# One-core attention with two feed-forward layers: value matmuls a step later, evacuations by kind, another order of the first two head pairs

## The chip, the cores and the metric

The kernel runs on one core of one Trainium2 chip. The metric is the device time of one execution in microseconds (us); for the kernel before it is the median of three runs. Engine names: TensorE (PE, its weight loads PEld), VectorE (DVE), ScalarE (ACT), GpSimd (POOL) and SyncE (SP), which here issues all DMA transfers from one queue (SPq).

## The reference

Four batches of eight heads are given, 576 positions, 64 channels a head, all float32. Queries and keys are rotated by position, attention is computed, and its output (2304 tokens by 512 channels) passes through two feed-forward layers of width 2048.

```python
def rotate(x):
    x1, x2 = (x[..., :half], x[..., half:])
    return np.concatenate([x1 * cos - x2 * sin, x1 * sin + x2 * cos], axis=-1)
...
scores = scale * np.matmul(rotate(q), rotate(k).transpose(0, 1, 3, 2))
scores = scores - np.max(scores, axis=-1, keepdims=True)
attn = np.exp(scores)
attn = attn / (np.sum(attn, axis=-1, keepdims=True) + 1e-09)
x = np.matmul(attn, v)             # then laid out as 2304 x 512
h = x @ w_in;  x = np.where(h > 0, h, np.exp(np.minimum(h, 0)) - 1) @ w_out
h = x @ w_in2; x = (h - np.tanh(h)) @ w_out2
```

## The kernel before, in words

**Two stages.** The attention stage handles 16 pairs of heads. The feed-forward stage (from L428) works through two layers in 192 steps. Both are written as loops whose program order is kept on each engine. The change lies in the attention stage, but for one constant (`NCV`) that both stages use.

**Items and steps.** A pair has nine items: eight score tiles of 128 queries by 576 keys (four tiles of each head), and a ninth that holds the last 64 queries of both heads. The main loop (L378) makes step i out of parts of different items. In its order, step i issues: the loads scheduled for i; `emit_max(i)`, the row maximum of score tile i (VectorE); `emit_s(i+1)`, the matmuls of the next score tile; `emit_exp(i)`, the exponential with its row sum (ScalarE); `flush()`, which copies to SBUF what the step before left in PSUM; `emit_norm(i-1)`, after every second item the reciprocals (VectorE) and the scaling of two tiles (GpSimd, L251); the `prep` parts scheduled for i; at some steps a part of a weight conversion (`conv_w`); `emit_t(i-4)`, four TensorE transposes, with one more for the remaining 64 columns (`pr`); and the value matmuls (`emit_pv`) that fall due, as `PV_AT` says, one, two or three steps after their last transposes. In this text "step r of a pair" counts i modulo nine.

**Buffers that tie steps together.** Score tiles have two PSUM buffers, so `emit_s(i+1)` waits for the exponential of item i-1. Transposes have three PSUM buffers and the value result has one. Normalised tiles have three SBUF buffers; rotated inputs `t`, keys `k` and values have two.

**Preparing a pair.** `load_qk(p, x)` loads queries (x=0) or keys (x=1) with their swapped halves into `t` (576 KB in one transfer). `prep(p, x, i)` then has five parts: i=0 and 1 multiply the two halves by the tables (GpSimd; for pair 0 and half of pair 1 VectorE); 2 adds them (VectorE, L148); 3 makes the rounded high part (ScalarE, L151); 4 makes the low part (VectorE, L156) and issues the copies that `place` makes of both parts: four of 288 KB for keys (`k<-hl`), four of 144 KB for queries (`qa<-hl`, `qb<-hl`). The score matmuls of a pair read these copies. Only the first `NDIRECT` score tiles read the rotated float32 tiles directly (L193). `when` and `early` say in which step each load and part is issued. Rotated tiles have two buffers each, so the tiles of pair 2 take the place of those of pair 0.

**Weights.** `load_w` loads a 512 KB block of raw 8-byte weights, `conv_w` turns it into two float32 parts: ScalarE takes an absolute value, VectorE makes four instructions, ScalarE and GpSimd split the result. One block is converted in every two pairs.

**Evacuations.** `evac` notes copies of transposes to SBUF (nine of 512 columns and five of 128 or 64 in each pair), and `flush` gives two of every five to VectorE and the others to ScalarE, by a running count, whatever their size.

Of the kernel before, what the change touches and what calls it, by code (L numbers as in the profile page):

```python
# [8 lines left out]
F32 = mybir.dt.float32  # L9
# [3 lines left out]
ALU = mybir.AluOpType  # L13
# [10 lines left out]
def attention_elu_tanhshrink(ctx: ExitStack, tc: tile.TileContext, qk, v, w1i, w1o, w2i, w2o, tab, out):  # L24
# [6 lines left out]
    nc = tc.nc  # L31
    NPAIR = qk.shape[0]
    NTOK, DM = out.shape
    S = 576
    NB = 384
    SCALE = 0.125
# [31 lines left out]
        raw_t[key] = t  # L68

    cv_t = {}  # L70
    NCV = 5

    def conv_w(key, slot, part):
        l, kind, c = key
        if part < 4:
            words = raw_t[key].bitcast(U32).rearrange("p (n t) -> p n t", t=2)
            lo_w, hi_w = words[:, :, 0], words[:, :, 1]
        if part == 0:
            cv_t[key] = cv_p.tile([128, 512], F32, tag="f", name="f")
        f = cv_t[key]  # L80
        fu = f.bitcast(U32)
        if part == 0:
            nc.scalar.activation(out=f, in_=hi_w.bitcast(F32), func=AF.Abs)
        elif part == 1:
            nc.vector.tensor_scalar(out=f, in0=f, scalar1=LO_CLAMP, scalar2=HI_CLAMP, op0=ALU.max, op1=ALU.min)
            nc.vector.tensor_scalar(
                out=fu, in0=fu, scalar1=3, scalar2=0x3FFFFFFF, op0=ALU.logical_shift_left, op1=ALU.bitwise_and
            )
        elif part == 2:
            nc.vector.scalar_tensor_tensor(  # L90
                out=fu, in0=hi_w, scalar=0xC0000000, in1=fu, op0=ALU.bitwise_and, op1=ALU.bitwise_or
            )
        elif part == 3:
            nc.vector.scalar_tensor_tensor(
                out=fu, in0=lo_w, scalar=29, in1=fu, op0=ALU.logical_shift_right, op1=ALU.bitwise_or
            )
            raw_t.pop(key)
        else:
            w = w_pools[slot // 4 if slot < 4 else -1].tile(
                [128, 2, 512], F32R, tag=f"w{kind}_{slot}", name=f"w{kind}_{slot}"  # L100
            )
            nc.scalar.copy(out=w[:, 0, :], in_=f)  # L102
            nc.gpsimd.tensor_tensor(out=w[:, 1, :], in0=f, in1=w[:, 0, :].bitcast(F32), op=ALU.subtract)  # L103
            w_t[key] = w
            cv_t.pop(key)


    with ExitStack() as actx:
# [27 lines left out]
        def prep(p, x, i):  # L136
            t = t_t[p, x]
            mul = SCALE if p > 0 and x == 0 else 1.0
            if i < 2:
                if p == 0 and x == 0:  # L140
                    nc.vector.scalar_tensor_tensor(
                        out=t[:, i, :], in0=t[:, i, :], scalar=SCALE, in1=tabs[:, i, :], op0=ALU.mult, op1=ALU.mult
                    )
                else:
                    eng = nc.vector if p < 2 and i == 1 else nc.gpsimd
                    eng.tensor_tensor(out=t[:, i, :], in0=t[:, i, :], in1=tabs[:, i, :], op=ALU.mult)  # L146
            elif i == 2:
                nc.vector.tensor_tensor(out=t[:, 0, :], in0=t[:, 0, :], in1=t[:, 1, :], op=ALU.add)  # L148
            elif i == 3:
                hl_t[p, x] = p1.tile([128, 2, S], F32R, tag=f"hl{x}", name=f"hl{x}")  # L150
                nc.scalar.mul(hl_t[p, x][:, 0, :], t[:, 0, :], mul)  # L151
            else:
                hl = hl_t.pop((p, x))
                if p > 0:
                    t_t.pop((p, x))
                nc.vector.scalar_tensor_tensor(  # L156
                    out=hl[:, 1, :], in0=t[:, 0, :], scalar=mul, in1=hl[:, 0, :].bitcast(F32),
                    op0=ALU.mult, op1=ALU.subtract,
                )
                if p == 0 and x == 0:  # L160
                    first_hl.append(hl)
                for h in range(2):
                    if p > 0:
                        place(p, x, h, hl)
                    elif x == 1:
                        place(p, 0, h, first_hl[0])
                        place(p, 1, h, hl)

        first_hl = []

        def place(p, x, h, hl):
            src = hl[64 * h:64 * h + 64].bitcast(F32)
# [79 lines left out]
                    out=a, in0=a, scalar1=r[:, x:x + 1], scalar2=1.0, op0=ALU.mult, op1=ALU.mult  # L252
                )

        ev = [0]
        late, late_x = [], []

        def evac(out_, in_):
# [1 line left out]

        def flush():
            for out_, in_ in late:
                ev[0] += 1
                if ev[0] % 5 in (1, 3):
                    nc.vector.tensor_copy(out_, in_)  # L265
                else:
                    nc.scalar.copy(out_, in_)  # L267
            late.clear()
            for p, grp, o, n in late_x:
                b, hp = divmod(p, 4)  # L270
                x0 = NTOK * hp + b * S + 256 * grp
                nc.scalar.copy(out=xa[:, x0:x0 + n], in_=o[:, 0:n])
            late_x.clear()
# [58 lines left out]
                late_x.append((p, min(grp, 1), o_t.pop((p, min(grp, 1))), 256 if grp == 0 else 320))  # L332

        D = 4
        NDIRECT = 2
        NI = 9
        first_w = [(0, kind, c) for c in range(NJ) for kind in range(2)]
        sched = {}
        early = {1: ((None, 0, 0, 1, 2, 3), (None, 0, 0, 0, 1, 2)), 2: ((0, 4, 5, 7, 7, 8), (4, 7, 9, 11, 12, 13))}
        for p in range(1, NPAIR):  # L340
            i0 = NI * (p - 1)
            for x in range(2):
# [3 lines left out]
                if when[0] is not None:  # L346
                    sched.setdefault(when[0], []).append((load_qk, p, x))
                for k in range(5):
                    sched.setdefault(when[k + 1], []).append((prep, p, x, k))
            sched.setdefault(i0 + 7, []).append((load_v, p))  # L350
        with tc.manual_schedule():
            for x in range(2):
                t = t_t[0, x] = p2.tile([128, 2, S], F32, tag=f"t{x}", name=f"t{x}")
                for i in range(2):
                    nc.sync.dma_start(out=t[:, i, :], in_=qk[0, :, 2 * x + i, :])
                    if x == 0:
                        nc.sync.dma_start(out=tabs[:, i, :], in_=tab[:, i, :])
            load_qk(1, 0)
            load_qk(1, 1)
            load_v(0)  # L360
            make_identity(nc, ident)
            nc.vector.memset(zero, 0.0)
            for i in range(2):
                nc.scalar.copy(out=qa_t[i][:, S:640], in_=zero)
                nc.scalar.copy(out=qb_t[i][:, 0:64], in_=zero)
            for i in range(3):
                prep(0, 0, i)
            for i in range(3):
                prep(0, 1, i)
            n = len(items)  # L370
            pend = []
            nw = list(range(len(first_w)))[::-1]
            emit_s(0)
            PV_AT = ((1, 1, 1, 3, 3), (1, 1, 1, 3, 3), (2, 2, 2, 2, 2))
            for i in range(3, 5):
                for x in range(2):
                    prep(0, x, i)
            for i in range(n + D + 1):  # L378
                p, r = divmod(i, NI)
                for f, *arg in sched.get(i, ()):  # L380
# [13 lines left out]
                if p < NPAIR:  # L394
                    for f, *arg in sched.get(i, ()):
                        if f is prep:
                            f(*arg)
                    c = NI * (p % 2) + r - 3
                    if c >= 0 and c % 2 == 0 and c // 2 < NCV and p // 2 < len(first_w):
                        key = first_w[p // 2]  # L400
                        conv_w(key, key[2], c // 2)
                if 0 <= i - D < n:
                    emit_t(i - D)
                    pp, uu, hh = items[i - D]
# [214 lines left out]
```

## Time and profile before

| what | us |
|---|---|
| median of three runs (1132.15 to 1132.97) | 1132.17 |
| profiled execution, its own time | 1132.65 |
| span of that execution in the trace | 1130.9 |
| PE busy in the span | 1097.3 |
| DVE busy | 765.6 |
| ACT busy | 688.6 |
| POOL busy | 671.3 |

The span runs from the first to the last instruction of the trace; the execution's own time has 1.75 us more around it. Busy times are sums over instructions. A busy PE is not PE at its peak, since the ends of pipelined matmuls are modelled. Times in the rows below count from the start of the span.

### The profile page before, as it was taken

Reading aid. Unit: us, or ns where it says so; the run is one execution under the profiler, and the core shown is the slowest. Engines: PE = TensorE matmul, PEld = TensorE weight load, DVE = VectorE, ACT = ScalarE, POOL = GpSimd, SP = SyncE. Lnnn points to the kernel's source line nnn. Section 1 sums busy time; section 2 is a strip of 40 time slices with the busy share of each in tenths; the row PEclk is TensorE's granted clock in tenths of the full one; section 3 lists DMA queues with packets and bytes.
Section 4 is the critical chain, followed back from the end, with each engine's and each line's share of the span. In section 5 each row is a group of like instructions: output and inputs, shape, how many; then the busy total and the mean of one; then the engine's idle time right before and its main releaser. Section 6 shows DMA issues by size and latency. Waiting matters only on the chain.

```text
span 1130.9 us, 18518 instructions
## 1 busy us (share of the span) xinstructions
PE 1097.3 (97%) x6656; PEld 987.2 (87%) x6656; DVE 765.6 (68%) x1393; ACT 688.6 (61%) x1477; POOL 671.3 (59%) x609
## 2 busy tenths in 40 slices
PE   2899999999999999999999999999999999999998
PEld 2777776777799999999999999998998899899987
DVE  6988888888645434555545556678768877877665
ACT  3676766676745533333333344688888788877774
POOL 2877887887556533333333466676666666666443
PEclk9999999999999999999999999999999999999999
DMA  7767676865211111112111121111111111110102
GB/s 232 217 193 200 181 215 169 222 172 164 72 39 38 40 55 38 38 38 55 40 38 38 38 57 38 39 38 38 57 38 38 38 56 38 38 39 1 57 35 78
DMA packets 29627, 91.96 MB, mean 81 GB/s; under 512 B 4192, under 2 KB 4192, under 8 KB 29536
## 3 DMA queue, kind: packets, MB, share of 16 engines
q1 hardware_dynamic: 29536, 90.78, 28.3%
q8 instruction: 53, 0.87, 0.3%
q14 instruction: 38, 0.31, 0.1%
HBM read 57.74 MB, written 4.72 MB: 55 GB/s over the span
## 4 chain that ended last, share of the span: by engine, by line
PE 90%; DVE 5%; DMA 2%; ACT 2%; SPq 1%; issue 1%; ACTq 0%; DVEq 0%
PE h L445 36%; PE y L503 18%; PE y L505 17%; PE o L325 8%; PE s L211 6%; PE pt L291 4%; DVE nm L220 2%; DMA k<-hl 1%; ACT a L234 1%; DVE t L148 1%; DVE aT L265 1%; ACT aT L267 1%; DVE hl L156 0%; DMA tabs<-in_tab 0%; PE pr L304 0%
## 5 line engine op out<-in xcount | busy, mean ns | idle before, releaser
L445 PE MATMUL h<-x,w 128*128 128x384 f32 x2304 | 434.0, 336 | 0.0
L445 PEld LDWEIGHTS h<-x,w 128*128 128x128 f32 x2304 | 407.1, 188 | 8.0 <-ACT a L234 0.4
L488 POOL TENSOR_TENSOR g<-f,g 128x384 fp32r<-128x384 f32 x192 | 213.6, 1113 | 187.8 <-ACT g L487 182.5
L503 PE MATMUL y<-g,w 128*128 128x384 f32 x1152 | 219.0, 339 | 0.0
L505 PE MATMUL y<-w,g 128*128 128x512 f32 x864 | 216.7, 395 | 0.2 <-ACT xa L520 0.2
L503 PEld LDWEIGHTS y<-g,w 128*128 128x128 f32 x1152 | 204.0, 188 | 0.0
L505 PEld LDWEIGHTS y<-w,g 128*128 128x128 f32 x864 | 161.5, 188 | 31.9 <-ACT xa L520 0.6
L251 POOL TENSOR_SCALAR a<-a,r 128x576 f32<-128x576 f32 x144 | 135.2, 951 | 63.7 <-DVE r L248 43.6
L464 POOL TENSOR_TENSOR w<-w,u 128x384 f32<-128x384 f32 x96 | 105.4, 1098 | 99.7 <-ACT w L463 99.7
L234 ACT ACTIVATE a<-s,nm 128x576 f32<-128x576 f32 x144 | 107.1, 743 | 89.6 <-DVE nm L220 75.1
L487 ACT CAST g<-f 128x384 fp32r<-128x384 f32 x192 | 98.0, 510 | 94.1 <-PE y L503 92.4
L475 DVE TENSOR_SCALAR f<-f 128x384 f32<-128x384 f32 x96 | 40.0, 416 | 145.4 <-ACT f L456 145.4
L456 ACT ACTIVATE f<-h 128x384 f32<-128x384 f32 x96 | 47.2, 492 | 146.7 <-PE h L445 143.8
L220 DVE TENSOR_REDUCE nm<-s 128x1 f32<-128x576 f32 x144 | 108.2, 753 | 38.1 <-PE s L211 36.5
L103 POOL TENSOR_TENSOR w<-f,w 128x512 fp32r<-128x512 f32 x64 | 82.6, 1291 | 54.4 <-ACT w L102 54.3
L522 DVE TENSOR_TENSOR xa<-y,xa 128x384 f32<-128x384 f32 (+1 forms) x126 | 74.0, 612 | 47.3 <-PE y L503 42.0
L479 DVE TENSOR_TENSOR f<-h,f 128x384 f32<-128x384 f32 x96 | 53.1, 553 | 68.3 <-ACT f L465 67.8
L481 DVE COPY_PREDICATED f<-mask,w 128x384 f32<-128x384 uint32 x96 | 92.2, 961 | 10.3 <-DVE w L480 0.5
L325 PE MATMUL o<-aT,v 128*64 128x256 f32 (+1 forms) x768 | 89.3, 339 | 2.6 <-ACT aT L267 2.4
L146 POOL TENSOR_TENSOR t<-t,tabs 128x576 f32<-128x576 f32 x59 | 86.3, 1463 | 8.2 <-DMA t<-in_qk 8.2
L291 PE MATMUL pt<-ident,a 128*128 128x128 f32 x576 | 88.3, 277 | 0.1
L461 ACT ACTIVATE u<-h 128x384 f32<-128x384 f32 x96 | 47.4, 494 | 66.4 <-PE h L445 52.1
(55 smaller groups left out, 1379.2 us busy)
## 6 DMA issues: line engine op xcount, KB each, us to landing
k<-hl SPq DMA_DIRECT2D x64, 288.0 KB, 4.2
t<-in_qk SPq DMA_DIRECT2D x30, 576.0 KB, 6.2
raw<-in_w1i SPq DMA_DIRECT2D x16, 512.0 KB, 3.7
raw<-in_w1o SPq DMA_DIRECT2D x16, 512.0 KB, 3.7
raw<-in_w2i SPq DMA_DIRECT2D x16, 512.0 KB, 3.6
raw<-in_w2o SPq DMA_DIRECT2D x16, 512.0 KB, 3.6
v<-in_v SPq DMA_DIRECT2D x16, 288.0 KB, 4.7
qa<-hl SPq DMA_DIRECT2D x32, 144.0 KB, 4.0
```

The costliest lines, as they stand in the source:

```text
L220: nc.vector.tensor_reduce(out=nm, in_=s_t[i][:, :, 0:288], axis=AX.XY, op=ALU.max, negate=True)
L234: nc.scalar.activation(out=a.rearrange("p (x c) -> p x c", x=2), in_=s[:, :, 0:288], func=AF.Exp, bias=nm_t.pop(i), scale=1.0, accum_out=den,)
L251: nc.gpsimd.tensor_scalar(out=a, in0=a, scalar1=r[:, x:x + 1], scalar2=1.0, op0=ALU.mult, op1=ALU.mult)
L291: nc.tensor.transpose(pt[:, c, :], a[:, h or 0, c0:c0 + 128], ident)
L325: nc.tensor.matmul(out=o[sl, 0:n], lhsT=w, rhs=m, start=(c == 0), stop=(c == 4))
L445: nc.tensor.matmul(out=hp, lhsT=w[:, wp, ws], rhs=x_t[t][:, xp, c, :], start=(m == 0), stop=(m == 3 * KC - 1))
L464: nc.gpsimd.tensor_tensor(out=w, in0=w, in1=u, op=ALU.mult)
L481: nc.vector.copy_predicated(f, mask.bitcast(U32), w)
L487: nc.scalar.copy(out=g[:, 0, :], in_=f)
L488: nc.gpsimd.tensor_tensor(out=g[:, 1, :], in0=f, in1=g[:, 0, :].bitcast(F32), op=ALU.subtract)
L503: nc.tensor.matmul(out=y_t[e][:, 0:NB], lhsT=w[:, wp, es], rhs=gt[:, gp, :], start=st, stop=sp)
L505: nc.tensor.matmul(out=y_t[e], lhsT=gt[:, gp, es], rhs=w[:, wp, :], start=st, stop=sp)
```

## The change

The value matmuls of each group are issued one step later (`PV_AT`), and the load of a pair's values three steps later. Evacuations of at most 128 columns go to VectorE, all larger ones to ScalarE. The part of `conv_w` that held two VectorE instructions is cut in two, and the parts get their own steps (`CV_AT`, counted in 18 steps, two pairs). In the first pair VectorE does all products and sums: keys first, then queries 0 to 319, and after the first score matmuls are issued the other 256 queries. Keys and the first 320 queries are loaded ahead of the rest. The first four score tiles instead of two read float32. All four products of pair 1 go to GpSimd ahead of the loop, and the loads of pair 2 move from steps 0 and 4 to steps 4 and 5, its query parts by a step or two.

```diff
-    NCV = 5
+    NCV = 6
...
             nc.vector.tensor_scalar(out=f, in0=f, scalar1=LO_CLAMP, scalar2=HI_CLAMP, op0=ALU.max, op1=ALU.min)
+        elif part == 2:
             nc.vector.tensor_scalar(
                 out=fu, in0=fu, scalar1=3, scalar2=0x3FFFFFFF, op0=ALU.logical_shift_left, op1=ALU.bitwise_and
             )
...
             if i < 2:
-                if p == 0 and x == 0:
-                    nc.vector.scalar_tensor_tensor(
-                        out=t[:, i, :], in0=t[:, i, :], scalar=SCALE, in1=tabs[:, i, :], op0=ALU.mult, op1=ALU.mult
-                    )
-                else:
-                    eng = nc.vector if p < 2 and i == 1 else nc.gpsimd
-                    eng.tensor_tensor(out=t[:, i, :], in0=t[:, i, :], in1=tabs[:, i, :], op=ALU.mult)
+                nc.gpsimd.tensor_tensor(out=t[:, i, :], in0=t[:, i, :], in1=tabs[:, i, :], op=ALU.mult)
...
-                if p == 0 and x == 0:
-                    first_hl.append(hl)
                 for h in range(2):
-                    if p > 0:
-                        place(p, x, h, hl)
-                    elif x == 1:
-                        place(p, 0, h, first_hl[0])
-                        place(p, 1, h, hl)
+                    place(p, x, h, hl)
+
+        def rotate_first(x, cols):
+
+            t = t_t[0, x][:, :, cols]
+            for i in range(2):
+                if x == 0:
+                    nc.vector.scalar_tensor_tensor(
+                        out=t[:, i, :], in0=t[:, i, :], scalar=SCALE, in1=tabs[:, i, cols], op0=ALU.mult, op1=ALU.mult
+                    )
+                else:
+                    nc.vector.tensor_tensor(out=t[:, i, :], in0=t[:, i, :], in1=tabs[:, i, cols], op=ALU.mult)
+            nc.vector.tensor_tensor(out=t[:, 0, :], in0=t[:, 0, :], in1=t[:, 1, :], op=ALU.add)
...
-                ev[0] += 1
-                if ev[0] % 5 in (1, 3):
+                if out_.free_size() <= 128:
                     nc.vector.tensor_copy(out_, in_)
                 else:
                     nc.scalar.copy(out_, in_)
...
-        NDIRECT = 2
+        NDIRECT = 4
+        Q0 = 320
+        CV_AT = (3, 5, 7, 9, 10, 13)
-        early = {1: ((None, 0, 0, 1, 2, 3), (None, 0, 0, 0, 1, 2)), 2: ((0, 4, 5, 7, 7, 8), (4, 7, 9, 11, 12, 13))}
+        early = {1: ((None, None, None, 3, 3, 4), (None, None, None, 1, 1, 2)), 2: ((4, 5, 6, 7, 8, 9), (5, 7, 9, 11, 12, 13))}
...
-            sched.setdefault(i0 + 7, []).append((load_v, p))
+            sched.setdefault(i0 + 10, []).append((load_v, p))
...
+            for i in range(2):
+                nc.sync.dma_start(out=t_t[0, 1][:, i, :], in_=qk[0, :, 2 + i, :])
+                nc.sync.dma_start(out=tabs[:, i, :], in_=tab[:, i, :])
+                nc.sync.dma_start(out=t_t[0, 0][:, i, 0:Q0], in_=qk[0, :, i, 0:Q0])
+            nc.sync.dma_start(out=t_t[0, 0][:, :, Q0:S], in_=qk[0, :, 0:2, Q0:S])
+            load_qk(1, 1)
             load_qk(1, 0)
-            load_qk(1, 1)
             load_v(0)
...
-            for i in range(3):
-                prep(0, 0, i)
-            for i in range(3):
-                prep(0, 1, i)
+            rotate_first(1, slice(0, S))
+            rotate_first(0, slice(0, Q0))
...
             emit_s(0)
-            PV_AT = ((1, 1, 1, 3, 3), (1, 1, 1, 3, 3), (2, 2, 2, 2, 2))
-            for i in range(3, 5):
-                for x in range(2):
-                    prep(0, x, i)
+            PV_AT = ((2, 2, 2, 4, 4), (2, 2, 2, 4, 4), (3, 3, 3, 3, 3))
+            rotate_first(0, slice(Q0, S))
+            for x in (1, 0):
+                for i in range(2):
+                    prep(1, x, i)
+            prep(0, 1, 3)
+            prep(0, 1, 4)
+            prep(0, 0, 3)
+            sched.setdefault(0, []).insert(0, (prep, 0, 0, 4))
...
-                    c = NI * (p % 2) + r - 3
-                    if c >= 0 and c % 2 == 0 and c // 2 < NCV and p // 2 < len(first_w):
-                        key = first_w[p // 2]
-                        conv_w(key, key[2], c // 2)
+                    key = first_w[p // 2]
+                    if i % (2 * NI) in CV_AT:
+                        conv_w(key, key[2], CV_AT.index(i % (2 * NI)))
```

## Rows read from the trace of the kernel before

**Rows 1.** Windows by stage: start:end, length, busy PE, PEld, DVE, ACT, POOL, clock, DMA

```profile
0.00:41.12 41.12, 17.57 (x89) 13.84 (x90) 28.36 (x48) 15.75 (x35) 17.95 (x21) 0.96 0.83 242
41.12:53.16 12.04, 12.04 (x109) 9.12 (x108) 11.15 (x23) 8.10 (x22) 11.77 (x12) 1.00 0.58 162
53.16:306.67 253.51, 247.53 (x2047) 187.75 (x2045) 211.64 (x481) 176.65 (x440) 200.97 (x186) 1.00 0.67 180
318.71:1130.90 812.19, 808.21 (x4317) 768.52 (x4317) 510.80 (x833) 482.96 (x967) 437.42 (x388) 1.00 0.14 42
```

**Rows 2.** Windows of three single pair periods, same columns

```profile
180.55:199.59 19.04, 17.62 (x148) 13.40 (x147) 16.52 (x36) 12.80 (x32) 16.30 (x16) 1.00 0.65 186
199.59:217.18 17.59, 17.59 (x148) 13.41 (x147) 14.58 (x36) 12.33 (x31) 13.09 (x12) 1.00 0.78 200
289.22:306.67 17.45, 17.45 (x149) 13.39 (x147) 11.94 (x32) 12.53 (x32) 11.12 (x13) 1.00 0.21 59
```

**Rows 3.** Timeline, PEld: ninth score tile of pairs 1 and 15 (16 such rows)

```profile
53.16 0.81 PEld L211 LDWEIGHTS s<-k,qb 128*128 128x128 f32 x6
...
306.67 0.81 PEld L211 LDWEIGHTS s<-k,qb 128*128 128x128 f32 x6
```

**Rows 4.** Chain of waits, 181 to 186 us: start, length, what

```profile
181.26 1.70 DVE f L90
...
182.96 0.68 DVE nm L220
...
183.67 0.83 ACT a L234 x2
...
184.50 0.48 ACT aT L267
...
185.03 1.51 PE o L325 x10
```

**Rows 5.** Waits of PEld, 40 to 308 us: total, times, longest

```profile
PEld o L325 <- ACT aT L267: 8.2, 14, 1.9
```

**Rows 6.** Timeline of the start: start, length, instruction (idle before, releaser)

```profile
7.73 1.99 DVE L148 TENSOR_TENSOR t<-t 128x576 f32<-128x576 f32 x1
...
9.77 3.75 POOL L146 TENSOR_TENSOR t<-t,tabs 128x576 f32<-128x576 f32 x2 [0.66 <-DMA t<-in_qk]
...
10.50 1.76 DVE L148 TENSOR_TENSOR t<-t 128x576 f32<-128x576 f32 x1
...
12.19 2.62 DVE L156 SCALAR_TENSOR_TENSOR hl<-t,hl 128x576 fp32r<-128x576 f32 x2
...
12.32 2.30 PE L193 MATMUL s<-t,t 64*128 64x288 f32 x8 [12.32 <-DVE t L148]
...
14.73 0.74 DVE L220 TENSOR_REDUCE nm<-s 128x1 f32<-128x576 f32 x1
...
14.84 1.10 SPq L178 DMA_DIRECT2D k<-hl  x2
```

**Rows 7.** Timeline, later: pair 2's query products, score tiles 10 and 11

```profile
29.18 2.96 POOL L146 TENSOR_TENSOR t<-t,tabs 128x576 f32<-128x576 f32 x2
...
40.04 0.81 PE L211 MATMUL s<-k,qb 128*128 128x288 f32 x4
...
41.12 0.57 PEld L211 LDWEIGHTS s<-k,qa 128*128 128x128 f32 x4
```

**Rows 8.** Second pair of key copies: issues (ns, start), then us to landing

```profile
L178 SPq DMA_DIRECT2D k<-hl x2: 595/598/600, 18.3 to 19.0; - x2
DMA to landing us min/median/max: 3.8/4.2/4.6
```

**Rows 9.** Windows with the DMA engines full: of copies, of loads

```profile
8.00:10.00 2.00, 0.00 (x0) 0.00 (x0) 2.00 (x2) 0.24 (x1) 1.34 (x2) 1.00 1.02 415
...
22.00:24.00 2.00, 0.30 (x1) 0.34 (x2) 0.12 (x1) 0.32 (x1) 1.46 (x2) 1.00 0.90 214
```

**Rows 10.** Groups by line and shape, 40 to 310 us: GpSimd's scaling

```profile
L251 POOL TENSOR_SCALAR a<-a,r 128x576 f32<-128x576 f32 x136 | 128.4, 955 | 49.3 <-DVE r L248 29.3 <-ACT a L234 15.9 <-ACT aTr L267 3.9
```

More of the change, by code (lines that the diff above doesn't have):

```diff
@@ L70, in attention_elu_tanhshrink @@
     cv_t = {}
-    NCV = 5
+    NCV = 6
     def conv_w(key, slot, part):
         l, kind, c = key
-        if part < 4:
+        if part < 5:
             words = raw_t[key].bitcast(U32).rearrange("p (n t) -> p n t", t=2)
@@ L88, in conv_w @@
             )
-        elif part == 2:
+        elif part == 3:
             nc.vector.scalar_tensor_tensor(
@@ L92, in conv_w @@
             )
-        elif part == 3:
+        elif part == 4:
             nc.vector.scalar_tensor_tensor(
@@ L159, in prep @@
                 )
-                if p == 0 and x == 0:
-                    first_hl.append(hl)
                 for h in range(2):
-                    if p > 0:
-                        place(p, x, h, hl)
-                    elif x == 1:
-                        place(p, 0, h, first_hl[0])
-                        place(p, 1, h, hl)
-        first_hl = []
+                    place(p, x, h, hl)
[9 more added lines that the diff above has]
+            nc.vector.tensor_tensor(out=t[:, 0, :], in0=t[:, 0, :], in1=t[:, 1, :], op=ALU.add)
         def place(p, x, h, hl):
@@ L253, in emit_norm @@
                 )
-        ev = [0]
         late, late_x = [], []
@@ L348, in attention_elu_tanhshrink @@
                 for k in range(5):
-                    sched.setdefault(when[k + 1], []).append((prep, p, x, k))
-            sched.setdefault(i0 + 7, []).append((load_v, p))
+                    if when[k + 1] is not None:
+                        sched.setdefault(when[k + 1], []).append((prep, p, x, k))
+            sched.setdefault(i0 + 10, []).append((load_v, p))
         with tc.manual_schedule():
             for x in range(2):
[L353 to L357, printed above, removed]
+                t_t[0, x] = p2.tile([128, 2, S], F32, tag=f"t{x}", name=f"t{x}")
+            for i in range(2):
[4 more added lines that the diff above has]
+            load_qk(1, 1)
             load_qk(1, 0)
-            load_qk(1, 1)
             load_v(0)
```

## The prediction

> **What bounds the kernel now.** I read the windows by stage first. From 318.71 us on, the feed-forward stage keeps PE busy for 808.2 of 812.2 us [rows 1]. The change only regroups its conversion parts (the same instructions, still one block in three steps), and the 4 us that PE lacks lie mostly at the end of the span. I count this stage as unchanged.
>
> The attention stage ends at 318.71 and has two regimes. I number score tiles from 0, as the code does. Up to 41.12 us, where tile 11 starts and step 9 ends on PE, PE is busy for 17.57 us only; this is the start, with DMA busy at 0.83 [rows 1]. From the last score tile of pair 1 (tile 17, its ninth; 53.16) to that of pair 15 (306.67) lie 14 periods in 253.51 us [rows 1, 3], 18.11 us each. A period without preparation of a later pair takes 17.45 us with PE busy throughout; one with all of it takes 17.59 [rows 2]. So 17.45 is the floor of PE's program, and at most 14 x (18.11 - 17.45) = 9.2 us are to be had in steady state. The reader should see who takes them: in a period of 19.04 us, the chain runs from a conversion instruction (1.70, L90) over the maximum, the exponential and a ScalarE evacuation into the value matmuls [rows 2, 4]. Value matmuls waited for evacuations 14 times, 8.2 us in all [rows 5]. The rest of the chain after 306.67 stays in the same order.
>
> **Steady state, part by part.** Later value matmuls: at step 8 they need an evacuation that stands behind that step's exponential; a step later it is done. This removes the waits of [rows 5]. Large evacuations all on ScalarE: 9 instead of 5.4 in each pair, 3.6 x 0.48 = 1.7 us more work [rows 4], less some small ones, on an engine busy for 12.3 to 12.8 us of a period [rows 2]; it stays under 15 of 17.45, hidden under PE. VectorE gets about as much less.
>
> What is late next: without value matmuls, step 8 is short on PE. The second tile of the next pair needs the exponential of the ninth tile, which follows that tile's matmuls by 0.76 + 0.83 + gaps = 1.7 us (maximum as in [rows 6, 4]); PE has about 1.6 us of other work meanwhile. That is a tie, if VectorE is punctual. After it VectorE has reciprocals, a low part, a maximum and, in every second pair, two conversion instructions at steps 0 and 1, all in order ahead of later maxima. When these meet GpSimd's products, each can wait for one (0.6 or so becomes 1.70 [rows 4]). From step 8 to step 2 of such a pair I add some 7 us of VectorE work (five maxima at 0.74 [rows 6], low part and sum at as much, two conversions of 0.6, small things) and 1 to 2 us of such waiting, against 4/9 of 17.45 = 7.8 us of PE's work in four steps: a stall of 0.2 to 1.2, I take 0.7. So, as estimates, a period with conversions in this stretch comes to 18.2 us and the other kind to 17.5, mean 17.85. Gain 14 x 0.26 = 3.6 us, with 0 and 9.2 as bounds. Moving the value loads frees the queue of a wait that blocks copies behind it; no copy is awaited by PE in the steady rows, so I count nothing, and a late key copy is a rival below.
>
> **The start.** Three things get earlier. Keys are rotated first on VectorE alone. In the rows, a sum takes 1.99 and 1.76 us beside GpSimd's products and PE starts at 12.32 [rows 6]; the maximum over as many columns takes 0.74, and at that price for each product and sum, and 0.42 for 320 of 576 columns of the queries, PE would start near 10.3 (the second table lands later by the 160 KB put ahead of it). Four direct tiles mean that the third and fourth score tile don't wait for key copies.
>
> But the gain stops at VectorE's queue. Between the first score matmuls and the first maximum now stand three operations on the other 256 queries and the keys' low part. At that time all four products of pair 1 run on GpSimd, from about 9.77, when pair 1's first tile landed before [rows 6]; as many bytes are ahead of it now. How the two engines share is in [rows 6]: the sum that began at 7.73 ended 0.6 after GpSimd's product, the products at 9.77 took 3.75 for two instead of 1.4 each, and VectorE's sum and low part between them ended after each product in turn. They alternate, one instruction each. So four products (1.26 to 1.4 each, 5.2) with three short VectorE operations between (256/576 of 0.6, 0.27 each) run from 10.2 to 16.0, and the low part of the keys ends at 16.55, against 14.81 before (14.84, first key copy [rows 6]). The first maximum follows at 16.6, against 14.73: later by 1.9, though PE starts 2 earlier. Bounds: if VectorE were never held up, the low part would end at 10.2 + 1.1 + 0.75 = 12.1; if it lost every turn, at 17.3. I take 16.55, which the rows show.
>
> The Trainium skill (SBUF — State Buffer, Who interferes with whom) says that a VectorE instruction with two SBUF inputs and a GpSimd instruction that reads SBUF exclude each other, that the one issued later blocks fully, and that a reduction does not contend. The trace agrees: the sums took 1.76 and 1.99, the maximum 0.74 [rows 6]. By that rule the sum for the low part is the same as by the rows, and the rule speaks against putting four products there.
>
> From 16.55 the copies set the pace. Copies between buffers moved 214 GB/s with the DMA engines full, loads 415 [rows 9]. Ahead of pair 2's query tile now stand pair 0's copies (1152 + 576 KB), a weight block (512 KB), and pair 1's key copies (1152 KB), because its load went from step 0 to step 4. 2880 KB of copies take 13.8 us, 1088 KB of loads 2.7. The first start needs 1.9 us more (before: 14.84 to 23.6, where 18.99 + 4.6 landed the last key copy [rows 6, 8], 8.8 us for 1440 KB that take 6.9 at that rate). The tile lands near 16.55 + 13.8 + 2.7 + 1.9 = 35.0.
>
> What is queued behind it: GpSimd's product at step 5 (1.4) waits for it, then stand two scalings (0.95 each, [rows 10]) and the second product (1.4): 39.7. VectorE's sum at step 7 waits for that, perhaps behind one more product (0 to 1.4, I take 0.7), and takes 0.76; behind it a conversion instruction (0.45, an estimate well under the 1.70 in [rows 4]) and then tile 8's maximum (0.76), whose exponential (0.83) frees the buffer for tile 10. Tile 10 starts at 43.2, against 40.04 [rows 7], where both products were done by 32.14. Step 9 then needs the rest as before (41.12 - 40.04 = 1.08) and the value matmuls that it now holds (1.45, from 1.51 in [rows 4]): 45.7 against 41.12 at the same point of the work, 4.6 later. After such a pause I add 1.3 for PE's clock, which was below full in part of the first 41 us (0.96 on the mean [rows 1]), and for VectorE, which has pair 1's conversions and the delayed sums to catch up: 5.9. From there both kernels have the same work, 12.04 in the rows with PE busy throughout [rows 1]. Bounds of the loss: 0, with the low part at 12.1; 7.5, with every turn lost.
>
> **Sum.** 5.9 - 3.6 = 2.3 us later. The profiled execution took 1132.65, 0.5 over the median of the runs; against the median: 1132.2 + 2.3 = 1134.5. I take 0.2% (2.3 us) as what a measurement of this kernel tells from no change, so the forecast stands at that edge, on the slower side.
>
> **The rivals.** A, the forecast: the start loses 4 to 7, the periods gain 2 to 5. 1131.5 to 1138, chance 0.45 (0.28 slower, 0.15 within 0.2%, 0.02 faster).
>
> B, the periods come down to 17.5. For it: PE is busy for nearly all of [rows 1], its waits are those that the later value matmuls remove, and 17.59 was reached with all preparation running [rows 2]. Against it: VectorE's order from step 8 to step 3. Gain 8.5, loss 5: 1128.7. It decides from a mean period of 18.11 - 5.9/14 = 17.69 downwards. Chance 0.25 (0.18 faster, 0.07 within).
>
> C, GpSimd's four products don't hold VectorE: its short operations pass between two products together. For it: nothing in [rows 6] shows so short ones. Against it: each full one there lost its turn. Copies then start near 13, pair 2's tile lands at 31.5, the loss is about 1: 1132.2 + 1 - 3.6 = 1129.6. Chance 0.13 (0.09 faster, 0.04 within). The skill, in the section named above, says that issue order decides who blocks; this is how it could come out that way.
>
> D, a new wait in steady state: with the short step 8 the second tile of a pair comes 1 to 2 us sooner after the keys' low part, and its key copies, whose last landed 4.6 us after issue [rows 8], arrive late. The periods gain nothing: 1132.2 + 5.9 = 1138.1. Against it: no steady row of PE waits for copies. Chance 0.12, slower.
>
> E, both effects are small: 1132, chance 0.05.
>
> Together: faster 0.29, within 0.2% 0.31, slower 0.40. The range 1126.5 to 1139 takes in B with a smaller loss at the start and D with a larger one; beyond it lie the floor of 17.45 with no loss (1123) and the top loss with nothing gained (1139.7).
>
> **What would show it.** Right: the first maximum after 16; GpSimd idle for some 5 us until pair 2's query tile lands near 35; VectorE's sum of pair 2 waiting for GpSimd; tile 10 after 42; pair 1's last score tile near 59; periods of 17.5 and 18.2 in turn; no value matmuls waiting for evacuations. Wrong: low part of the keys before 14, or that marker under 55 (the start), or a mean period under 17.7 (steady state).

## The result, and the profile after

The changed kernel takes 1142.06 us (median of 4 runs, 1141.37 to 1143.97), the kernel before 1132.22 on the same chip: ratio 1.0087 [1.0076, 1.0099], 9.8 us slower. The forecast was 1134.5 with a range to 1139. The profiled execution of after is the slowest of the four, 1143.97, with a span of 1142.1; so its rows overstate the typical loss by about 1.5.

The windows by stage of after, cut at the same points of the work as [rows 1] (tile 11 starts on PE; last score tile of pair 1; of pair 15; start of the feed-forward stage). Columns as in [rows 1].

```profile
0.00:51.46 51.46, 21.84 (x90) 15.99 (x90) 29.02 (x50) 17.42 (x39) 20.73 (x23) 0.91 0.65 185
51.46:64.23 12.77, 12.70 (x107) 9.42 (x106) 8.44 (x21) 7.95 (x19) 10.04 (x10) 0.97 0.78 213
64.23:318.18 253.95, 247.13 (x2047) 186.16 (x2046) 184.83 (x471) 194.87 (x454) 203.09 (x186) 1.00 0.66 179
...
330.20:1142.10 811.90, 807.90 (x4315) 767.97 (x4314) 498.65 (x830) 482.12 (x966) 426.59 (x388) 1.00 0.14 42
```

Tile 11 comes at 51.46 instead of 41.12 (10.3 later), pair 1's last score tile at 64.23 instead of 53.16 (11.1 later). The 14 periods take 253.95 instead of 253.51, the feed-forward stage 811.9 instead of 812.2. In these two traces the whole loss lies in the start, and the steady part, which was to win 3.6, wins nothing.

The timeline of after's start (start, length, instruction, idle time before it and releaser):

```profile
10.81 6.17 POOL L141 TENSOR_TENSOR t<-t,tabs 128x576 f32<-128x576 f32 x4 [9.50 <-DMA t<-in_qk]
11.02 3.16 DVE L163 SCALAR_TENSOR_TENSOR t<-t,tabs 128x256 f32<-128x256 f32 x2
...
14.21 1.50 DVE L168 TENSOR_TENSOR t<-t 128x256 f32<-128x256 f32 x1
15.64 1.96 DVE L151 SCALAR_TENSOR_TENSOR hl<-t,hl 128x576 fp32r<-128x576 f32 x1
...
17.62 3.45 SPq L177 DMA_DIRECT2D k<-hl  x4
...
25.22 0.68 ACT L146 ACTIVATE hl<-t 128x576 fp32r<-128x576 f32 x1 [4.76 <-DMA k<-hl]
...
26.73 4.04 SPq L177 DMA_DIRECT2D k<-hl  x4
...
30.86 0.65 SPq L129 DMA_DIRECT2D t<-in_qk  x1
31.11 1.33 PE L210 MATMUL s<-k,qa 128*128 128x288 f32 x4 [0.65 <-ACT a L233]
31.61 1.51 SPq L180 DMA_DIRECT2D qa<-hl  x2
...
38.28 1.40 POOL L141 TENSOR_TENSOR t<-t,tabs 128x576 f32<-128x576 f32 x1 [6.74 <-DMA t<-in_qk]
...
42.52 1.93 DVE L143 TENSOR_TENSOR t<-t 128x576 f32<-128x576 f32 x1 [7.26 <-POOL t L141]
...
46.37 1.33 PE L210 MATMUL s<-k,qb 128*128 128x288 f32 x4 [5.26 <-ACT a L233]
...
48.70 2.83 PE L322 MATMUL o<-aT,v 128*64 128x256 f32 x12
...
51.46 0.85 PEld L210 LDWEIGHTS s<-k,qa 128*128 128x128 f32 x4 [0.76 <-ACT aT L264]
```

Read it as one chain. VectorE's three short operations (two products from 11.02, a sum at 14.21) take 1.5 to 1.6 each beside GpSimd's four products; the keys' low part ends, and the first copies issue, at 17.6. The first query product of pair 2 waits for its tile until 38.28; VectorE's sum waits for the products, tile 8's maximum stands behind the sum, tile 10 needs that tile's buffer and starts at 46.37. Then step 9 takes 5.1 us, because PE is at half clock. Two-microsecond windows of the same stretches:

```profile
14.00:16.00 2.00, 0.00 (x0) 0.00 (x0) 1.97 (x3) 0.25 (x1) 2.00 (x2) 1.00 0.00 0
...
42.00:44.00 2.00, 0.00 (x0) 0.00 (x0) 1.48 (x1) 0.00 (x0) 1.84 (x2) 0.50 0.02 7
...
50.00:52.00 2.00, 2.00 (x10) 1.02 (x7) 1.27 (x1) 0.84 (x3) 0.73 (x1) 0.50 0.86 199
52.00:54.00 2.00, 2.00 (x19) 1.83 (x17) 1.38 (x5) 0.56 (x1) 0.16 (x1) 0.97 0.97 282
```

The last three columns are the granted clock, the DMA share and GB/s. No DMA engine moves anything from 14 to 16 (nor from 16 to 18): the copies wait for VectorE. From 42 to 52 the granted clock is 0.50 (the level of 1.2 GHz).

What PE's weight loads waited for between 64 and 318 us in after (total, times, longest), beside [rows 5]:

```profile
PEld s L210 <- ACT aT L264: 14.0, 32, 1.4
PEld s L210 <- ACT a L233: 13.9, 34, 1.0
```

The value matmuls' waits for evacuations of [rows 5] are gone, as forecast. Score matmuls now wait for ScalarE in their place. (Waits of the loads overlap PE's work in part, so they are not a sum of lost time.)

### The profile page after: what moved, and what is told of

Its sections match the earlier page's. It is cut to its first block, busy times and chain, and to the rows that moved or that the text cites. A ratio compares the mean times of both kernels' runs of the same rounds, so it can differ in the third digit from the quotient of the medians.

```text
span 1142.1 us, 18512 instructions
## 1 busy us (share of the span) xinstructions
PE 1101.5 (96%) x6656; PEld 987.7 (86%) x6656; DVE 723.4 (63%) x1385; ACT 707.6 (62%) x1487; POOL 663.7 (58%) x610
## 4 chain that ended last, share of the span: by engine, by line
PE 82%; DVE 8%; DMA 4%; POOL 2%; ACT 2%; issue 1%; SPq 1%; DVEq 0%; ACTq 0%; POOLq 0%
PE h L448 34%; PE y L506 17%; PE y L508 17%; PE o L322 5%; PE s L210 5%; DVE nm L219 3%; PE pt L288 2%; DMA t<-in_qk 2%; DMA k<-hl 1%; DVE hl L151 1%; DVE f L95 1%; POOL a L250 1%; SPq L177 1%; POOL t L141 1%; DVE t L143 1%
## 5 line engine op out<-in xcount | busy, mean ns | idle before, releaser
L491 POOL TENSOR_TENSOR g<-f,g 128x384 fp32r<-128x384 f32 x192 | 206.7, 1077 | 196.8 <-ACT g L490 193.5
L250 POOL TENSOR_SCALAR a<-a,r 128x576 f32<-128x576 f32 x144 | 138.9, 977 | 65.0 <-DVE r L247 64.8
L467 POOL TENSOR_TENSOR w<-w,u 128x384 f32<-128x384 f32 x96 | 101.4, 1056 | 102.9 <-ACT w L466 102.9
L85 DVE TENSOR_SCALAR f<-f 128x512 f32<-128x512 f32 x64 | 28.0, 438 | 165.7 <-ACT f L83 165.7
L264 ACT COPY aT<-pt 128x512 f32<-128x512 f32 x144 | 83.9, 585 | 1.8 <-PE pt L288 1.8
L322 PE MATMUL o<-aT,v 128*64 128x256 f32 (+1 forms) x768 | 81.4, 341 | 0.0
```

The costliest lines, as they stand in the source:

```text
L250: nc.gpsimd.tensor_scalar(out=a, in0=a, scalar1=r[:, x:x + 1], scalar2=1.0, op0=ALU.mult, op1=ALU.mult)
L322: nc.tensor.matmul(out=o[sl, 0:n], lhsT=w, rhs=m, start=(c == 0), stop=(c == 4))
L467: nc.gpsimd.tensor_tensor(out=w, in0=w, in1=u, op=ALU.mult)
L491: nc.gpsimd.tensor_tensor(out=g[:, 1, :], in0=f, in1=g[:, 0, :].bitcast(F32), op=ALU.subtract)
```

## The experiments

**Which half loses.** The steady part alone, on the kernel before with its start (`conv_w` in six parts and its loop as in the change):

```diff
-    NCV = 5
+    NCV = 6
...
-                ev[0] += 1
-                if ev[0] % 5 in (1, 3):
+                if out_.free_size() <= 128:
...
+        CV_AT = (3, 5, 7, 9, 10, 13)
...
-            sched.setdefault(i0 + 7, []).append((load_v, p))
+            sched.setdefault(i0 + 10, []).append((load_v, p))
...
-            PV_AT = ((1, 1, 1, 3, 3), (1, 1, 1, 3, 3), (2, 2, 2, 2, 2))
+            PV_AT = ((2, 2, 2, 4, 4), (2, 2, 2, 4, 4), (3, 3, 3, 3, 3))
```

The new start alone is the changed kernel with all of these edits turned back, among them:

```diff
-            PV_AT = ((2, 2, 2, 4, 4), (2, 2, 2, 4, 4), (3, 3, 3, 3, 3))
+            PV_AT = ((1, 1, 1, 3, 3), (1, 1, 1, 3, 3), (2, 2, 2, 2, 2))
...
-                if out_.free_size() <= 128:
+                ev[0] += 1
+                if ev[0] % 5 in (1, 3):
```

> The kernel before with only the steady part of the change (later value matmuls, evacuations by kind, conversion cut into six parts, later value loads); its start is the old one. Theory 1, the whole loss is made in the start and the steady part is worth nothing: 1132 to 1133 us, last score tile of pair 1 near 53, mean pair period 18.1. Theory 2, the steady part loses too: above 1136. Theory 3, the steady part gains once it does not inherit the bad start (a mean period of 17.85 as forecast): near 1128.5.

> The changed kernel with the steady part taken back (value matmuls, evacuations by count, five conversion parts and value loads as before); its start is the new one. Theory 1: 1141 to 1143 us, last score tile of pair 1 near 64, mean period 18.1. Theory 2: 1136 or less. Theory 3: 1145.

Steady part alone: 1134.63 (before 1131.84; ratio 1.0027 [1.0016, 1.0038]), 2.8 slower. Start alone: 1140.76 (1.0081 [1.0057, 1.0105]), 8.9 slower, pair 1's last score tile at 62.67 and the periods as in the kernel before. The first fell between its theories 1 and 2. The four runs of the second lie 6 us apart (1138.09 to 1144.42), so its 8.9 is a rough figure. Still the start carries most of the loss, and the steady part is a small loss too, not a gain.

**Inside the start: the load or VectorE's order.** Two edits of the changed kernel, one at a time. In the first, pair 2's query tile is loaded right behind tile 3's matmuls, ahead of pair 1's key copies in SP's queue:

```diff
-        early = {1: ((None, None, None, 3, 3, 4), (None, None, None, 1, 1, 2)), 2: ((4, 5, 6, 7, 8, 9), (5, 7, 9, 11, 12, 13))}
+        early = {1: ((None, None, None, 3, 3, 4), (None, None, None, 1, 1, 2)), 2: ((None, 5, 6, 7, 8, 9), (5, 7, 9, 11, 12, 13))}
...
+                if i + 1 == NDIRECT - 1:
+                    load_qk(2, 0)
```

In the second, the keys' low part stands ahead of the other 256 queries on VectorE:

```diff
+            prep(0, 1, 3)
+            prep(0, 1, 4)
             rotate_first(0, slice(Q0, S))
...
-            prep(0, 1, 3)
-            prep(0, 1, 4)
```

> The changed kernel with one transfer moved: pair 2's query tile is loaded right behind the matmuls of score tile 3, ahead of pair 1's key copies, instead of behind them. If the order of the transfers makes the stall: the tile lands near 30 instead of 38.3, GpSimd's products of it are done by 35, tile 10 starts near 41 instead of 46.4 and PE's clock falls for less long: 1133 to 1136 us. If the late low part of the keys (VectorE behind GpSimd's products) makes it: at most 2 us gained, 1140 to 1142.

> The changed kernel with VectorE's low part of pair 0's keys issued ahead of the rotation of the other 256 queries. If the alternation with GpSimd's four products sets the start of the copies: low part done near 13.7 instead of 17.6, key copies 3.9 us earlier, pair 2's query tile near 34.4, tile 10 near 42.5: 1138 us. If only the order of the transfers counts: 1141 to 1142. If both are needed before anything moves: 1142.

Load ahead: 1134.85 (8 runs, 1131.9 to 1137.0; 1.0028 [1.0017, 1.0039]), 7.2 under the changed kernel. Low part ahead: 1139.37 (1.0066 [1.0051, 1.0081]), 2.7 under it. In the second the key copies issue at 10.96 instead of 17.62, and yet the timeline shows the same wait as before, shifted:

```profile
10.80 6.01 POOL L141 TENSOR_TENSOR t<-t,tabs 128x576 f32<-128x576 f32 x4 [9.50 <-DMA t<-in_qk]
10.85 3.17 DVE L163 SCALAR_TENSOR_TENSOR t<-t,tabs 128x256 f32<-128x256 f32 x2
...
32.71 1.40 POOL L141 TENSOR_TENSOR t<-t,tabs 128x576 f32<-128x576 f32 x1 [6.03 <-DMA t<-in_qk]
```

GpSimd still stands idle for 6 us until the tile lands. By the medians the position of one 576 KB load in SP's queue is the larger cause, VectorE's lost turns the smaller. The traces put the two closer together: with the low part ahead, pair 1's last score tile comes at 58.82, 5.4 earlier than in after, and the 14 periods give back 1.6 of that (255.56 against 253.95). The profile of the first kernel (its fastest run, 1131.9) is no clean test of the load alone: there GpSimd began its products at 11.34 instead of 10.81, and VectorE had passed its short operations by then (the key copies issue at 11.68 instead of 17.62). The spread of 5 us in this kernel's runs is wide enough to hold both orders; that it comes from them was not shown.

How many turns VectorE loses is not fixed by the program. Three kernels have the same order of instructions up to the first copies (the third follows below), and their profiles differ (times of start, us):

| kernel | VectorE's first product on the other 256 queries | GpSimd's first product | first key copies | first product of pair 2's query tile | pair 1's last score tile |
|---|---|---|---|---|---|
| after | 11.02 | 10.81 | 17.62 | 38.28 | 64.23 |
| start alone | 10.20 | 10.38 | 15.60 | 36.89 | 62.67 |
| conversion moved | 9.85 | 10.25 | 14.04 | 35.16 | 60.16 |

The rows of the third:

```profile
9.85 0.75 DVE L163 SCALAR_TENSOR_TENSOR t<-t,tabs 128x256 f32<-128x256 f32 x2
...
10.25 6.89 POOL L141 TENSOR_TENSOR t<-t,tabs 128x576 f32<-128x576 f32 x4 [8.95 <-DMA t<-in_qk]
...
14.04 3.46 SPq L177 DMA_DIRECT2D k<-hl  x4
```

The earlier VectorE begins against GpSimd, the fewer turns it loses, and 3.6 us at the first copies go with 4.1 us at pair 1's last score tile. The trace of after is the latest of the three.

**Inside the steady part: the two halves alone**, each on the kernel before: later value matmuls with the later value load; or evacuations by size. The first:

```diff
-            sched.setdefault(i0 + 7, []).append((load_v, p))
+            sched.setdefault(i0 + 10, []).append((load_v, p))
...
-            PV_AT = ((1, 1, 1, 3, 3), (1, 1, 1, 3, 3), (2, 2, 2, 2, 2))
+            PV_AT = ((2, 2, 2, 4, 4), (2, 2, 2, 4, 4), (3, 3, 3, 3, 3))
```

The second:

```diff
-                ev[0] += 1
-                if ev[0] % 5 in (1, 3):
+                if out_.free_size() <= 128:
```

> The kernel before with only the value matmuls a step later (and the value loads three steps later). If VectorE's order from step 8 to step 2 is the bound of every second period, with its share of large evacuations left on it: those periods near 18.9, the others 17.8, 1133 to 1135 us. If waiting for evacuations was what the periods lost: periods near 17.6, 1126 us.

> The kernel before with only the evacuations by kind (large ones on ScalarE, small ones on VectorE). If a relieved VectorE is worth something without later value matmuls: 1129 us. If the value matmuls then wait for ScalarE's evacuation behind the exponential in every pair (0.5 us or so each): 1134 to 1138 us.

Later value matmuls: 1132.66 (0.9999 [0.999, 1.0009]), nothing; that is just under the 1133 to 1135 of its first theory and far from the 1126 of the second. Evacuations by size: 1135.53 (1.0024 [1.0015, 1.0034]), 2.8 slower, and every period from 18.32 to 18.36. Its waits from 52 to 310 us:

```profile
PE o L324 <- ACT aT L266: 3.0, 13, 0.2
...
PEld o L324 <- ACT aT L266: 13.8, 28, 0.7
```

Twice in each of the 14 pairs a value matmul stands behind a ScalarE evacuation. By count, two of five went to VectorE and the phase changed from pair to pair; by size every pair meets the same wait. So this half needs the later value matmuls, and they find little to remove without it.

**The conversion at steps 0 and 1.** The changed kernel with the last three conversion parts and the weight load moved.

```diff
-        CV_AT = (3, 5, 7, 9, 10, 13)
+        CV_AT = (3, 5, 7, 14, 16, 17)
...
-                if i == 1 or i % (2 * NI) == 12:
+                if i == 1 or i % (2 * NI) == 17:
```

> The changed kernel with the last three conversion parts at counts 14, 16 and 17 of 18 (steps 5, 7 and 8 of every second pair) instead of 9, 10 and 13 (steps 0, 1 and 4), and the raw load behind them at 17. If VectorE's two conversion instructions at steps 0 and 1 make the 18.48 us of every second period: those fall to about 17.6, 7 x 0.88 = 6 us off, 1136 us. If the short step 8 by itself (its exponential before the next pair's second tile) makes it: nothing changes, 1142.

1137.72 (1.0047 [1.0032, 1.0063]), 4.3 under the changed kernel. In after, one such instruction meets a product and holds the next maximum; the timeline of one period of 18.49:

```profile
160.19 1.42 POOL L141 TENSOR_TENSOR t<-t,tabs 128x576 f32<-128x576 f32 x1
...
160.39 1.76 DVE L95 SCALAR_TENSOR_TENSOR f<-raw,f 128x512 uint32<-128x512 uint32 x1
...
162.08 0.74 DVE L219 TENSOR_REDUCE nm<-s 128x1 f32<-128x576 f32 x1
...
162.92 0.74 ACT L233 ACTIVATE a<-s,nm 128x576 f32<-128x576 f32 x1 [1.30 <-DVE den L246]
...
163.80 0.56 PEld L210 LDWEIGHTS s<-k,qa 128*128 128x128 f32 x4 [0.56 <-ACT a L233]
```

The groups of the last conversion instruction, 40 to 310 us (count, busy, mean ns), of after:

```profile
L95 DVE SCALAR_TENSOR_TENSOR f<-raw,f 128x512 uint32<-128x512 uint32 x8 | 13.3, 1667 | 0.0
```

and with the conversion moved:

```profile
L95 DVE SCALAR_TENSOR_TENSOR f<-raw,f 128x512 uint32<-128x512 uint32 x8 | 5.7, 710 | 0.0
```

In this kernel's profile the periods that were 18.48 came down to 17.58 and the others came up to 18.18: part of the stall moved to the next pair. All 14 take 250.80, 3.2 less than in after and not the 6 of the theory. The rest of this profile's gain is not the edit's: tile 10 starts at 43.25 against 46.37, and up to there the two programs are the same (the table above shows the race that differs). So the 4.3 is no clean price. The start of the kernel before gives a better one: 1134.63 with the steady part alone, 1129.32 with the conversion moved as well ("steady moved" below), 5.3 less.

**All three repairs together**: load ahead, low part ahead, conversion moved.

> The changed kernel with all three edits tried so far: pair 2's query tile loaded ahead of pair 1's key copies, the keys' low part ahead of the other 256 queries, and the conversion parts moved. If the causes are the three named and add up: 1134.9 of the run with the load ahead, less 6 for the periods and 1 to 2 for the low part: 1127 to 1128.5, faster than the kernel before. If the short step 8 holds the periods: 1133 to 1134.

1128.32 (4 runs, 1126.37 to 1129.87; before 1132.72; 0.9959 [0.9944, 0.9974]): 4.4 faster than before, the lowest time here. Pair 1's last score tile is at 51.22, and 14 periods take 250.23, 17.87 each, against 18.11. Four kernels are made from it. "By count" has the evacuations of before, as in the diff above turned back; "new start" has the whole steady part of before; "steady moved" has the start of before and the steady part of this kernel, which is the kernel with the steady part alone and the moved conversion. "Two products" puts pair 1's query products at step 0:

```diff
-        early = {1: ((None, None, None, 3, 3, 4), (None, None, None, 1, 1, 2)), 2: ((None, 5, 6, 7, 8, 9), (5, 7, 9, 11, 12, 13))}
+        early = {1: ((None, 0, 0, 3, 3, 4), (None, None, None, 1, 1, 2)), 2: ((None, 5, 6, 7, 8, 9), (5, 7, 9, 11, 12, 13))}
...
-            for x in (1, 0):
-                for i in range(2):
-                    prep(1, x, i)
+            for i in range(2):
+                prep(1, 1, i)
```

> The kernel with all three repairs (1128.32 us, pair 1's last score tile at 51.22, periods of 18.18 and 17.58 in turn), with one thing taken back: evacuations go by count again, two of five to VectorE. Theory: evacuations by kind cost the kernel before 2.8 us since ScalarE then holds back value matmuls; with value matmuls a step later that wait is gone, so the split matters little here: 1127.5 to 1129.5. Rival: the ScalarE load itself stalls PE in each pair (the exponential and the transposes behind it): then it is 2 to 3 us faster, near 1126, with a mean period below 17.8.

> The new start with its two repairs (pair 2's query tile loaded ahead of pair 1's key copies, the keys' low part ahead of the other 256 queries), and the whole steady part as in the kernel before. Theory: pair 1's last score tile near 51.2 against 53.16, periods as before (mean 18.1): 1 to 2 us faster than before, near 1130.5. Rival: the gain of the kernel with all three repairs came from the start alone: then this one reaches 1128.3 too.

> The kernel before with its own start, and the whole steady part of the change with the conversion's last three parts (and the weight load) moved as in the kernel with the conversion moved. Theory: the steady part pays only when no conversion instruction stands on VectorE at steps 0 and 1 of a pair: periods of 18.18 and 17.58 in turn (mean 17.88 against 18.11), pair 1's last score tile near 54: 1 to 4 us faster than before, near 1129.5. Rival: the gain of the kernel with all three repairs needs its start as well (what is loaded when carries on into the periods): then the periods stay near 18.1 and the time at 1132 to 1135.

> The kernel with all three repairs (1128.32 us, 1126.37 to 1129.87), with GpSimd's two products for pair 1's queries issued at step 0 and no longer ahead of the loop, so that VectorE's work on the other 256 queries meets two products instead of four. Theory: each VectorE instruction that stands beside the products waits for one of them, so fewer products mean fewer lost turns: the other 256 queries are done 1 to 3 us sooner, pair 1's last score tile at 49.5 to 51, 1126.5 to 1128. Rival: the queue of copies sets the start by then, or the products, now behind, make pair 1's queries late: pair 1's last score tile at 51 or later, 1128 to 1131.

| kernel | median, us | ratio to before |
|---|---|---|
| by count | 1133.70 | 1.0017 [1.0008, 1.0026] |
| new start | 1133.14 | 1.0011 [1.0002, 1.0020] |
| steady moved | 1129.32 | 0.9977 [0.9968, 0.9986] |
| two products | 1130.26 | 0.9984 [0.9975, 0.9993] |

By count and new start missed both the theory and the rival: neither is faster than before. The windows over the 14 periods show where the first loses; of the kernel with all three repairs:

```profile
51.22:301.45 250.23, 244.94 (x2047) 185.92 (x2045) 180.13 (x472) 194.71 (x454) 207.50 (x187) 1.00 0.67 182
```

and with evacuations by count:

```profile
52.80:308.01 255.21, 245.62 (x2047) 185.99 (x2046) 203.21 (x480) 177.54 (x444) 204.08 (x186) 1.00 0.65 179
```

By count VectorE has 23 us more and ScalarE 17 less, and the periods grow by 5.0 in all. Evacuations by size cost 2.8 alone and are worth some 5 here; which of VectorE's instructions then holds PE was not tried. Steady moved has the time of its theory, but not its periods: in its profile they take 18.02 on the mean and not 17.88 (52.37 to 304.65; the first three take 18.2 to 18.7). That is 1.2 us less than in the kernel before, and pair 1's last score tile comes 0.8 earlier. So on the old start the steady part with the conversion moved gives 2.9 of the best kernel's 4.4, while the repaired start alone gives nothing (pair 1's last score tile at 53.42 against 53.16). That the two together give more than the sum is measured, not explained. Two products left GpSimd's products where they were (still four in a row from 10.65 to 16.71, since nothing ahead of step 0 holds GpSimd back), so it doesn't test what it was meant to. It does show how the start varies. In the profile of the best kernel VectorE's two products on the other 256 queries took

```profile
10.36 1.96 DVE L163 SCALAR_TENSOR_TENSOR t<-t,tabs 128x256 f32<-128x256 f32 x2
```

and in that of two products, with the same order at this point,

```profile
10.75 3.16 DVE L163 SCALAR_TENSOR_TENSOR t<-t,tabs 128x256 f32<-128x256 f32 x2
```

With one turn more lost against GpSimd (1.2 us), pair 1's last score tile is at 53.89 instead of 51.22; that this turn makes all of the 2.7 is not shown. The program is the same up to there; GpSimd's products, which wait for a load, began 0.03 later than VectorE's first of the two in the best kernel and 0.10 earlier in the other (10.39 and 10.65).

## Why the prediction was wrong

**The start: right mechanism, mis-sized.** Predicted 5.9 later at pair 1's last score tile, measured 11.07. Two terms of the sum failed above all: the landing of pair 2's query tile (35.0, measured 38.28) and the term for PE's clock and VectorE (1.3, measured 3.3). By the steps of the prediction:

- The keys' low part ends at 17.6 (predicted 16.55; the first maximum follows at 17.52 instead of 16.6). VectorE and GpSimd do take turns as forecast: the two products took 3.16, the sum 1.50, the low part 1.96. GpSimd's four began at 10.81 instead of 10.2 and took 6.17 instead of 5.8 (the prediction's own terms add up to 6.0). That 16.55 came within 1.1 is in part luck: with the same order the low part ended at 15.6 and at 14.0 in the other two profiles of the table above.
- Pair 2's query tile lands at 38.28 (35.0). The later start is 1.0 of it. For the rest, the prediction added up what stands ahead of the tile in the queue: with the tile itself 3968 KB, 4.06 MB. From 18 to 38 us the DMA engines moved 4.7 MB (235 GB/s). Behind the tile's load (30.86) pair 1's query copies were issued (from 31.61, 576 KB, 0.59 MB), and from 34.45 two more loads. The row from which the prediction took 1.9 us for "the first start" shows the same: from 14.84 to 23.6 the kernel before moved 1.8 MB, while the 1440 KB of copies are 1.47 MB; loads issued from 19.68 on made the rest. The two stretches, first of before, then of after:

```profile
14.84:23.60 8.76, 1.30 (x4) 0.98 (x4) 5.11 (x10) 1.67 (x4) 1.29 (x2) 1.00 0.93 206
```

```profile
18.00:38.00 20.00, 13.04 (x52) 10.59 (x52) 10.30 (x24) 9.68 (x22) 3.71 (x4) 1.00 0.93 235
```

- The queue, then, orders the issues, and transfers in flight share the engines; that is read from sums, not tried. The high part of pair 1's keys also waited 4.76 for pair 0's copies to leave the one `hl` buffer. That the landing is what delays the start is shown by the load ahead, 7.2 faster by the medians.
- From the landing to tile 10 the prediction has 8.2, the trace 8.1 (38.28 to 46.37). The sum is right, and two of its terms are off in opposite directions: the scalings took 1.5 instead of 1.9, VectorE's sum 1.9 beside a product instead of 1.5.
- Step 9 was to take 2.5 and took 5.1 at half clock; up to pair 1's last score tile another 0.7 is lost. The prediction put 1.3 for the clock and for VectorE; it measured 3.3. Here the upper bound of 7.5 failed: the lost turns were in it, but the term for the clock stayed at 1.3.

6.3 (tile 10 against 40.04 in [rows 7]) + 4.0 (step 9 against 1.08) + 0.7 = 11.1.

**Steady state: the gain of 3.6 was nothing** (0.4 slower in these traces, just outside the lower bound of 0). Periods of 18.2 and 17.5 in turn were forecast; they came as 18.5 (the last, which prepares no pair, 17.59) and 17.6 to 18.6. The stall in a period with conversions was put at 0.7 and is 0.9 where the next one is undisturbed (18.48 against 17.58), with the conversion instruction at 1.67 on the mean, beside a product; with it moved these periods fall to 17.58. The other periods were to come to 17.5 and took 17.92 on the mean, three of seven 18.18 and more: this is the larger share of the error. Score matmuls behind ScalarE took the place of value matmuls behind ScalarE. Rival D is partly right: PE also waited three times on late transfers, 2.8 us in all. B needs 17.69 on the mean and was not near (18.14). C is refuted for this trace by the first rows of the timeline; in the profile of the conversion moved two of the short operations did get ahead of the products (9.85, 0.75 for both). The forecast mean of 17.85 was there to be had, as 17.87 in the best kernel shows, but only with the conversion away from steps 0 and 1, and not in full on the old start (18.02).

**The halves of the change are not a sum.** The prediction added the start and the periods; there that held roughly (8.9 + 2.8 = 11.7 against 9.8). Within the steady part it does not: evacuations by size cost 2.8 alone, later value matmuls nothing; the whole steady part costs 2.8 with the conversion at steps 0 and 1 and gains 2.9 with it moved.

The Trainium skill (SBUF — State Buffer, Who interferes with whom) has a VectorE instruction with two SBUF inputs contend with a GpSimd instruction that reads SBUF. The trace agrees: in the start, two-input instructions take 1.5 to 2.0 beside the four products. The maximum of 0.74 that the prediction set against this ran with GpSimd idle (its products ended at 13.52). A later one in the kernel before lies inside a product and takes 0.75:

```profile
37.35 1.80 POOL L146 TENSOR_TENSOR t<-t,tabs 128x576 f32<-128x576 f32 x1 [1.09 <-DMA t<-in_qk]
37.81 0.75 DVE L220 TENSOR_REDUCE nm<-s 128x1 f32<-128x576 f32 x1
```

What stays open: why every second period still takes some 18.18 in the kernels with the conversion moved, and what the wait for the `hl` buffer costs by itself, which was not tried. On the first the best kernel's profile has a lead: in four of these seven periods the conversion's first VectorE instruction (L85) takes 1.6 beside a product (0.42 in after), and in the other three PE waits 0.8 to 1.1 for the second tile of the pair.

## What to carry to other kernels

When a load moves to a later step, look at what its queue holds by then and at what the first instruction on it holds up: here one 576 KB load behind 1152 KB of copies was worth some 7 us by the medians, more than the work saved ahead of it. An instruction on VectorE that meets a GpSimd product can cost a product's time on top of its own (1.67 instead of 0.71 here), and PE pays for it only where a maximum that it needs stands behind: move it to a step where nothing waits. Try the parts of a change in each other's company, since a part that loses alone may be the one that makes the rest pay.

## What was not expected of the hardware

The half-clock level lasted from about 42 to 52 us in after. PE had worked for 1.4 of the 4.9 us ahead of it (37.0 to 41.9), stood still until 46.37, and then worked without a gap for 5.7 us before the clock rose. In the kernel before, the clock fell at 35.6, when PE was back at work after 3 us with none (31.1 to 34.1), and the level lasted 3.4 us. Value matmuls took 2.83 for 12 in it and 1.51 for 10 in [rows 4]. The clock column does not account for every slow matmul: the four at 31.11 took 1.33, as those at 46.37, with 1.00 in the column; from 34.97 on four took 0.81. What made them slow is not shown.

GpSimd's start, moved by some 0.1 to 0.6 us against VectorE's, decides turns of 1.2 us or more between them, and 3.6 us of the first copies' issue in the table above. With the load ahead, VectorE began 1.6 before GpSimd, and the copies were issued at 11.68 instead of 17.62.
